# A 4096-point convolution beside a GELU layer: the second transform stage in 64 × 64 quarters of TensorE, the turn between the inverse stages as VectorE block transposes, by channel halves

## The chip, the core and the metric

One Trainium2 core runs one program. TensorE (PE; its weight loads are PEld), VectorE (DVE), ScalarE (ACT), GpSimd (POOL) and the DMA queues of SyncE (SP) and POOL run side by side and wait for each other through semaphores. The metric is the device time of the core in microseconds, median of the timed runs; the profile shows one execution, whose span is a little shorter than its time.

## The reference

Two branches on the same input `u` (2048 positions, 512 channels), mixed by a gate of each position:

```python
g = _sigmoid((x * gate_w).sum(-1, keepdims=True))
...
P = jnp.exp(logdA[:, :, None] * l[None, None, :])
K = jnp.einsum("dn,dnl,dn->dl", Cc, P, dB).real
...
Yf = Uf * Kf[None, :, :, :]
y = irfft2(Yf, (1, 2 * L))[..., :L].T + u * Dskip
...
h = _gelu(jnp.einsum("bsd,df->bsf", x, w1) + b1)
b = jnp.einsum("bsf,fd->bsd", h, w2) + b2
return g * a + (1 - g) * b
```

Branch `a` (its result is `y`) is a long convolution of every channel with 2048 taps `K`, which come from a state-space model with 128 states; it is done by transforms of length 4096. Branch `b` is a dense layer of width 1792 with GELU. Everything is float32. (The lines of `irfft2` and `_gelu` are shortened.)

## The kernel before

The program has two parts. `front` (lines 296 to 1023) holds three streams of work that a planner in Python lays out: `dense()` computes branch `b` in 16 blocks of 256 positions (two halves of the hidden width), `taps()` builds `K` in 16 chunks of 32 channels and takes each chunk through the first transform stage, and `signal()` does the same for `u` in 16 pieces. Each task has an engine, a cost and a due time (`vec`, `act`, `mm`, `move`, lines 303 to 318); `Plan.run` (line 216) turns them into one order for each engine by a list schedule, and the tasks are issued in that order. The constants at the top (`T_0`, `K_0`, `D_EV` and so on) are due times; `PS = (2, 3, 1, 2)` gives the PSUM banks of the accumulators `acc`, of the hidden block `ph`, of the tap chunk `pk` and of the first stage `pu`.

`first_stage` (line 369) splits its source into a high and a low part of reduced precision (`s1h` by ACT, `s1l` by DVE), and multiplies in two row halves of TensorE: six products of 512 columns (line 384) into two `pu` banks. For the signal ACT copies each bank to `st` and SP stores it to the DRAM buffer `t2_d`; for the taps ACT copies each to `sk` with a step (line 662), and after every fourth chunk eight DMAs store `sk` to `t2_d` in runs of 64 elements (line 677).

`conv` (line 1026) is issued in the order of the text, each engine in program order. It runs a loop over 32 frequencies `n`. One step:

- `fetch` (7 steps ahead): SP loads `t2` (512 KB, 128 partitions, taps and signal side by side), every fourth step the matrices `cc`.
- `forward` (2 ahead): two products with 128 × 128 weights and 512 columns, `p2k` for the taps, `p2u` for the signal.
- `factors` (1 ahead): ACT copies the real and the imaginary half of `p2k` into both halves of `kr` and `ki`, four copies of 64 × 512.
- `product`: DVE forms the complex product: two multiplications of 128 × 512, one difference and one sum of 64 × 512.
- `inverse`: one product of 128 × 128 and 512 columns into `pa`.
- `turn` and `settle` (1 behind): ACT copies `pa` to `sa`; SP stores it to the DRAM buffer `t4_d`; the partition of the next stage is another axis, so after a group of steps POOL collects the group from DRAM (or, for the last four steps, straight from `sa`) into the big tile `t3`, 32 rows of 512.

After the loop, `rest` multiplies what `front` left over of the dense branch (`late`), and 16 rounds of two products with `g1t` (128 × 64 weights, 512 columns, line 1137) turn `t3` into the output positions; DVE adds the gated result to the dense part `mo`, which was loaded from `out`, and SP stores it.

`front` uses the pools `kp` and `ps`; `conv` uses `fp` and `ps_f`, whose tiles take the same SBUF bytes and PSUM banks in the order of their first use, each tile waiting for the old tiles in its place. A tag with `bufs=n` has `n` places, and a new tile waits until all uses of the tile `n` before it are over.

Of the kernel before, what the change touches and what calls it, by code (L numbers as in the profile page):

```python
# [9 lines left out]
F32 = mybir.dt.float32  # L10
# [7 lines left out]
P = 128  # L18
# [29 lines left out]
PS = (2, 3, 1, 2)  # L48
# [21 lines left out]

GROUPS = ((0, 8, 0, 4), (8, 8, 1, 4), (16, 8, 2, 4), (24, 4, 3, 8), (28, 1, 7, 32), (29, 1, 15, 32), (30, 1, 23, 32), (31, 1, 31, 32))
# [9 lines left out]


def slot_q():
    return [32 + m if m < 32 else 63 - m for m in range(64)]


def k0_order():
    return [8 * (n % 4) + n // 4 for n in range(32)]
# [14 lines left out]
def constants():  # L103
# [6 lines left out]
    k0 = np.arange(32)  # L110
    p = np.arange(32)
    q = np.asarray(slot_q())
    k1 = np.arange(64)
    qn = np.arange(64)

    er, ei = om(4 * (64 * np.outer(p, k0) + 16 * p[:, None]))

    f1 = np.zeros((2, 32, 32, 2, 2))
    for i in range(2):
        f1[i, :, :, 0, i] = er  # L120
        f1[i, :, :, 1, i] = ei
    f1h, f1l = split12(np.concatenate([f1.reshape(64, P)] * 2, 0))


    g1 = np.zeros((2, 2, 32, 2, 32))
    for i in range(2):
        g1[i, 0, :, i] = er.T / L
        g1[i, 1, :, i] = ei.T / L
    g1 = g1.reshape(4, 32, 64)
    rows = np.zeros((P, 64))  # L130
    for first, count, at, step in GROUPS:
        for i in range(count):
            for j in range(4):
                rows[at + step * (4 * i + j)] = g1[j, k0_order()[first + i]]
    g1 = rows


    f2 = np.zeros((32, 2, 64, 2, 64))
    g2 = np.zeros((32, 2, 64, 64, 2))
    for k in range(32):  # L140
        er, ei = om(4 * (q[:, None] * k + 32 * np.outer(q, k1)) + q[:, None])
        f2[k, 0, :, 0], f2[k, 1, :, 0], f2[k, 0, :, 1], f2[k, 1, :, 1] = er, -ei, ei, er
        er, ei = om(4 * (qn[None] * k + 32 * np.outer(k1, qn)) + qn[None])
        g2[k, 0, :, :, 0], g2[k, 1, :, :, 0] = er, ei
        g2[k, 0, :, :, 1], g2[k, 1, :, :, 1] = -ei, er
    g2 = g2.reshape(32, P, 32, 2, 2).transpose(0, 1, 3, 4, 2)
    c2 = np.stack([f2.reshape(32, P, P), g2.reshape(32, P, P)], 1)
    c2 = c2[k0_order()].reshape(8, 4, 2, P, P).transpose(0, 3, 1, 2, 4)
    c1 = np.concatenate([f1h, f1l], 1)
    return (  # L150
# [1069 lines left out]
```

## Time and profile before

| | us |
|---|---|
| three timed runs: lowest, median, highest | 573.89, 574.33, 576.38 |
| the profiled execution | 573.42 |
| its span in the trace | 571.6 |
| PE busy | 538.8 (94%) |
| DVE busy | 476.7 (83%) |
| ACT busy | 415.8 (73%) |
| granted TensorE clock, mean | 0.976 |

Busy time is the union of the instructions of an engine; a float32 product of TensorE appears as two records. Rows of a group read: line, engine, operation, output and inputs, shape, count, then busy time, mean nanoseconds of one, and idle time before it with its releaser. Rows of the chain that ended last read: start, duration, engine, tile, line. Rows of a stretch read: the stretch, its length, busy time and count of each engine, granted clock, share of the DMA engines, GB/s.

### The profile page before, as it was taken

To read this page: it belongs to the slowest core of one execution; us is meant where nothing else is said; L and a number is where in the kernel's file an instruction comes from. 1 tells how busy PE (TensorE), PEld (TensorE's weight loads), DVE (VectorE), ACT (ScalarE), POOL (GpSimd) and SP (SyncE) were. 2 spreads that over 40 slices of the span, in tenths; PEclk is the share of its full clock that TensorE was granted. 3 is DMA by queue.
4 is the path that set the end of the run, shared out by engine and by line. 5 is a ranking of instruction groups with operands and counts; after the bars stand their busy time and mean duration, and the time that the engine had idled before them with its cause. 6 is when DMAs were issued, how large, how long until landed. Compare 5 with 4: busy or idle time off the path is not lost.

```text
span 571.6 us, 11723 instructions
## 1 busy us (share of the span) xinstructions
PE 538.8 (94%) x4554; PEld 407.9 (71%) x4554; DVE 476.7 (83%) x876; ACT 415.8 (73%) x702; POOL 32.2 (6%) x69
## 2 busy tenths in 40 slices
PE   7859999999999999999999999999998999999636
PEld 6728788888787888888888889898986333333412
DVE  5899998998889989898998898988613999999216
ACT  4998766799675799987678867376546999999100
POOL 2000000000000000000110111011100000000200
PEclk9959999999999999999999999999999999999959
DMA  8969644242774342558622339222259999999957
GB/s 254 309 202 325 215 139 160 101 130 84 233 233 143 117 131 93 159 183 216 172 76 38 94 92 187 74 39 76 38 126 338 368 311 406 452 349 349 280 123 285
DMA packets 77668, 110.01 MB, mean 192 GB/s; under 512 B 39030, under 2 KB 42234, under 8 KB 77500
## 3 DMA queue, kind: packets, MB, share of 16 engines
q1 hardware_dynamic: 71756, 88.41, 46.2%
q0 software_dynamic: 5856, 20.85, 14.8%
q8 instruction: 36, 0.59, 0.4%
q14 instruction: 20, 0.16, 0.1%
HBM read 63.62 MB, written 44.57 MB: 189 GB/s over the span
## 4 chain that ended last, share of the span: by engine, by line
PE 82%; DMA 7%; ACT 5%; DVE 3%; issue 2%; SPq 0%; POOL 0%; POOLq 0%; DVEq 0%
PE pk L643 11%; PE acc L901 9%; PE ph L853 9%; PE ph L855 8%; PE ph L854 8%; PE acc L903 8%; PE acc L902 8%; PE pa L1076 6%; PE pu L384 4%; PE p2k L1049 4%; PE p2u L1050 4%; DMA t<-sa 3%; PE pb L1137 3%; DMA t_d<-sa 1%; DMA y<-in_w_dram 1%
## 5 line engine op out<-in xcount | busy, mean ns | idle before, releaser
L853 PE MATMUL ph<-xh,wh 128*128 128x256 f32 x448 | 128.0, 286 | 1.9 <-DVE wh L732 1.1
L855 PE MATMUL ph<-xh,wl 128*128 128x256 f32 x448 | 127.1, 284 | 0.6 <-DVE wl L736 0.5
L854 PE MATMUL ph<-xlo,wh 128*128 128x256 f32 x448 | 126.6, 283 | 0.0
L853 PEld LDWEIGHTS ph<-xh,wh 128*128 128x128 f32 x448 | 85.1, 190 | 8.0 <-issue 4.1
L901 PE MATMUL acc<-wh,hh 128*128 128x512 f32 x210 | 87.8, 418 | 0.6 <-ACT hh L873 0.6
L854 PEld LDWEIGHTS ph<-xlo,wh 128*128 128x128 f32 x448 | 85.1, 190 | 1.7
L855 PEld LDWEIGHTS ph<-xh,wl 128*128 128x128 f32 x448 | 85.1, 190 | 1.5 <-DVE wl L736 1.5
L902 PE MATMUL acc<-wl,hh 128*128 128x512 f32 x210 | 83.1, 396 | 0.0
L903 PE MATMUL acc<-wh,hl 128*128 128x512 f32 x210 | 83.1, 396 | 0.0
L870 ACT ACTIVATE ph<-ph,b1t 128x256 f32<-128x256 f32 x112 | 50.6, 452 | 28.3 <-PE ph L855 26.5
L643 PE MATMUL pk<-y,xc 128*32 128x64 f32 x2048 | 61.5, 290 | 0.0
L643 PEld LDWEIGHTS pk<-y,xc 128*32 128x32 f32 x2048 | 57.2, 136 | 4.0 <-issue 2.5
L901 PEld LDWEIGHTS acc<-wh,hh 128*128 128x128 f32 x210 | 39.8, 190 | 19.9 <-issue 11.9
L883 DVE TENSOR_TENSOR hl<-ph,hh 128x512 fp32r<-128x512 f32 (+1 forms) x62 | 38.2, 618 | 14.1 <-ACT hh L873 13.8
L903 PEld LDWEIGHTS acc<-wh,hl 128*128 128x128 f32 x210 | 39.8, 190 | 10.0 <-DVE hl L883 1.1
L607 DVE TENSOR_TENSOR y<-y,ea 128x64 f32<-128x64 f32 (+4 forms) x80 | 45.3, 566 | 0.4
L662 ACT COPY sk<-pu 128x512 f32<-128x512 f32 x32 | 33.9, 1130 | 15.4 <-PE pu L384 15.3
L902 PEld LDWEIGHTS acc<-wl,hh 128*128 128x128 f32 x210 | 39.9, 190 | 5.8
L873 ACT CAST hh<-ph 128x512 fp32r<-128x512 f32 (+1 forms) x62 | 33.0, 532 | 10.9 <-PE acc L902 9.1
L452 DVE TENSOR_TENSOR xt<-xc,zz 128x256 f32<-128x256 f32 (+2 forms) x48 | 37.2, 775 | 1.9 <-ACT xc L578 1.6
L1058 ACT COPY kr<-p2k 64x512 f32<-64x512 f32 x64 | 37.0, 578 | 2.1 <-PE p2k L1049 1.7
L1059 ACT COPY ki<-p2k 64x512 f32<-64x512 f32 x64 | 37.2, 581 | 1.2
(137 smaller groups left out, 952.9 us busy)
## 6 DMA issues: line engine op xcount, KB each, us to landing
t<-t_d SPq DMA_DIRECT2D x32, 512.0 KB, 7.6
t_d<-st SPq DMA_DIRECT2D x32, 256.0 KB, 3.2
t_d<-sk SPq DMA_DIRECT2D x32, 256.0 KB, 4.3
t_d<-sa SPq DMA_DIRECT2D x28, 256.0 KB, 5.5
mo<-out_dram SPq DMA_DIRECT2D x9, 512.0 KB, 9.0
ld<-in_xt_dram SPq DMA_DIRECT2D x16, 256.0 KB, 4.2
xh_d<-xh SPq DMA_DIRECT2D x8, 512.0 KB, 4.3
xl_d<-xlo SPq DMA_DIRECT2D x8, 512.0 KB, 6.2
```

What stands on the lines that cost most here:

```text
L452: vec(2 * m, lambda: vv.tensor_mul(t, a, br), due, [ka, *kb], [kt])
L607: nc.vector.tensor_mul(both(n, 64 - 3 * n, n), both(0, 64 - n, n), an)
L643: nc.tensor.matmul(pks[q][32 * j : 32 * j + 32, gg], x[:, r, :, ch], y[:, r, :, ch], start=(r == 0), stop=(r == 1), skip_group_check=True,)
L853: nc.tensor.matmul(p, h, xh[xk][:, d], start=(d == 0), stop=False)
L854: nc.tensor.matmul(p, h, xlo[xk][:, d], start=False, stop=False)
L855: nc.tensor.matmul(p, lo, xh[xk][:, d], start=False, stop=(d == 3))
L870: nc.scalar.activation(phs[q][:, n], phs[q][:, n], AF.Gelu_apprx_tanh, bias=b1t[:, f : f + 1])
L883: nc.vector.tensor_sub(lo, phs[q][:, 0:nf], hi.bitcast(F32))
L901: nc.tensor.matmul(a, h, wh[1][w], start=start, stop=False)
L902: nc.tensor.matmul(a, h, wl[1][w], start=False, stop=False)
L903: nc.tensor.matmul(a, l, wh[1][w], start=False, stop=(j == 3))
L1059: nc.scalar.copy(ki[h : h + 64], pk[64:128])
```

## The change

The second transform stage, the product, the inverse and the last stage are rearranged.

- The 4096-point transform is split the other way round: the first stage now has 64 frequencies, the second 32 points, so that real and imaginary parts of 32 points are 64 rows. All 64 × 64 products of `conv` use one of four quarters of TensorE: two row halves, two column halves.
- `conv` runs 16 steps: two channel halves `f` of 256 channels, eight groups `m` of four frequency pairs. A step loads 1 MB of `t2` with four DMAs of 32 partitions each, and in the first eight steps 0.46 MB of the matrices `ca`, which now stay.
- `taps` (8 products of 256 columns) and `signal` (two times 8: the second time with weights moved by 32 columns, which gives real and imaginary part exchanged) go into whole banks; `factors` is two copies, `product` two multiplications each time. The sums of the complex product are made by `inverse`, which adds up two products in PSUM: 16 products.
- `collect` copies the result into `ta[f]`; there is no store to DRAM and no collecting. `turn` is a block transpose on DVE, 64 channels at once (2048 elements per partition): for the first half four of them lie in the loop, behind steps 7, 8, 11, 12; for the second half four stand after the loop.
- The last stage of the first half is done in the loop (`mix_first`, two behind each of the steps 9, 10, 13, 14): ACT scales by the gate, POOL adds to `out` in DRAM. The second half is done at the end, with DVE and `mo` as before, but with 256 columns.
- `rest` stands between the loop and the last four turns.
- In `front`, the first stage of the taps becomes `first_stage_taps`: 24 products of 256 columns in four row tiles into three `pu` banks and the `pk` bank itself, four strided copies of 256 elements; `PS` is `(2, 2, 1, 3)`. The stores to `t2_d` have runs of 256 (signal) and 128 (taps) elements. The due times are unchanged.

The diff, cut to its core:

```diff
-PS = (2, 3, 1, 2)
+PS = (2, 2, 1, 3)
...
+        def first_stage_taps(src, key, due, evac):
+            hi, lo, reads = split1(src, key, due)
+            banks = [(pus[q], ("pu", q)) for q in (take("pu", N_PU) for _ in range(3))]
+            banks.append((src, key))
...
+                todo = [(b, w, x) for b in range(2) for w, x in ((0, hi), (0, lo), (1, hi))]
+                for i, (b, w, x) in enumerate(todo):
+                    for j, (z, _) in enumerate(banks):
+                        r = slice(32 * j, 32 * j + 32)
+                        nc.tensor.matmul(
+                            z[:, 0:HD], c1t[r, 2 + 2 * b + w], half(x, r, b), start=(i == 0), stop=(i == 5)
+                        )
...
+        ca = pool.tile([P, 32, 224], F32, name="ca", bufs=1)
+        ta = [pool.tile([P, 32, HD], F32, name=f"ta{f}", bufs=1) for f in range(2)]
+        tb = pool.tile([P, 32, P], F32, name="tb", bufs=1)
...
+        def fetch(s):
+            f, m = divmod(s, 8)
+            if f == 0:
+                nc.sync.dma_start(ca[:, 4 * m : 4 * m + 4], c2[m])
+            t2s[s] = pool.tile([P, 4, 2, HD], F32, tag="t2", name=f"t2{s}", bufs=3)
+            for i in range(4):
+                nc.sync.dma_start(
+                    t2s[s][32 * i : 32 * i + 32], t2_d[f, m, i].rearrange("n q w d -> q n w d")
+                )
...
+        quarters = [(n, h, h, h ^ n) for n in range(2) for h in range(2)]
+        def forward(s, w, at, zs):
+            for p in range(2):
+                cs = slice(HD * p, HD * p + HD)
+                for n, h, r, c in quarters:
+                    j = 2 * p + n
+                    nc.tensor.matmul(
+                        zs[h][part(c), cs], ca[part(r), 4 * (s % 8) + j, at : at + 64],
+                        t2s[s][part(r), j, w], start=True, stop=True,
+                    )
...
+        def product(s, i):
+            for h, z in enumerate(pus.pop((s, i))):
+                w = pool.tile([P, D], F32, tag=f"w{i}{h}", name=f"w{s}{i}{h}", bufs=2 - i)
+                nc.vector.tensor_mul(w, z, fac[s][h])
...
+        def inverse(s):
+            pas[s] = [bank("pa", f"pa{s}{r}", 2) for r in range(2)]
+            for p in range(2):
...
+                            nc.tensor.matmul(
+                                pas[s][r][part(h), cs],
+                                ca[part(r), 4 * (s % 8) + 2 * p + n, 96 + 64 * i : 160 + 64 * i],
+                                prod[s, i][h][part(r), cs], start=(i == 0), stop=(i == 1),
+                            )
...
+        def turn(dst, d, src, e, n):
+            nc.vector.transpose(
+                dst[:, :, d : d + n].rearrange("p q d -> p d q"),
+                src[:, :, e : e + n].rearrange("p n d -> p d n"),
+            )
...
+        def mix_first(d, t):
+            z = bank("pb", f"pb{d}{t}", 1)
+            last(z, tb, 2 * t, 4, P)
+            ob = pool.tile([P, 4, P], F32, tag="ob", name=f"ob{d}{t}", bufs=2)
+            for i in range(4):
+                nc.scalar.mul(ob[:, i], z[:, P * i : P * i + P], gate[:, 0, t + i : t + i + 1])
...
+        for s in range(-1, 16):
+            if s < 15:
+                if s + 1 == 0:
+                    taps(1)
+                    factors(1)
+                signal(s + 1, 0)
+                product(s + 1, 0)
+                if 0 <= s and s + 2 < 16:
+                    taps(s + 2)
+                    factors(s + 2)
+                signal(s + 1, 1)
+                product(s + 1, 1)
+                if s >= 0 and s + 3 < 16:
+                    fetch(s + 3)
...
+            if s >= 0:
+                inverse(s)
+                collect(s)
+            if s in (7, 8, 11, 12):
+                i = (s + 1) % 2
+                turn(tb, 64 * i, ta[0], 64 * (i + 2 * (s // 10)), 64)
+            if s in (9, 10, 13, 14):
+                d = P * (s // 12)
+                for t in (0, 4) if s in (9, 13) else (8, 12):
+                    mix_first(d, t)
+        rest()
+        for d in range(0, HD, 64):
+            turn(ta[0], d, ta[1], d, 64)
+        for t in range(0, 16, 2):
+            z = bank(("pa", "pu")[t // 2 % 2], f"pz{t}", 2 + t // 2 % 2)
+            last(z, ta[0], 2 * t, 2, HD)
...
+                nc.vector.scalar_tensor_tensor(
+                    mo[:, i % 8], z[:, HD * (i - t) : HD * (i - t) + HD], gate[:, 0, i : i + 1], mo[:, i % 8],
+                    ALU.mult, ALU.add,
+                )
```

The tile `pk` has two banks, `pu` three (two taken by each `signal`), `pa` two, `pb` one. `w0` has two buffers per half, `w1` one.

More of the change, by code (lines that the diff above doesn't have):

```diff
@@ L129, in constants @@
[L129 to L145, printed above, removed]
@@ L150, in constants @@
+    c2 = c2.reshape(8, 4, P, 224).transpose(0, 2, 1, 3)
     return (
@@ L1092, in turn @@
[L1092 to L1108 removed]
+        t2s, pks, pus, fac, prod, pas = {}, {}, {}, {}, {}, {}
@@ L1109, in rest @@
                 first = s not in accs
-                last = not any(e[0] == s for e in late)
                 if first:
-                    accs[s] = ps.tile([P, D], F32, tag="pk", name=f"acc{s}", bufs=2)
+                    accs[s] = bank("pk", f"acc{s}", 2)
                 ss = slice(s * P, (s + 1) * P)
```

258 lines of the change are left out of this document (120 added, 138 removed).

## The prediction

> **What bounds the kernel now.** I read the page's head first, then the busy time by stretch of the span, then the chain that ended last.
>
> ```profile
> span 571.6 us, 11723 instructions
> core 0: us, PE busy (x) PEld busy (x) DVE busy (x) ACT busy (x) POOL busy (x), PEclk, DMA share, GB/s
> 0.00:436.30 436.30, 423.10 (x4256) 361.13 (x4256) 377.20 (x729) 325.88 (x542) 27.42 (x61) 0.98 0.52 150
> 436.30:523.10 86.80, 85.51 (x183) 32.28 (x184) 79.04 (x119) 82.96 (x148) 1.59 (x3) 1.00 1.00 379
> 523.10:551.60 28.50, 14.69 (x52) 9.19 (x51) 8.49 (x13) 6.92 (x13) 3.24 (x5) 0.82 0.91 241
> 551.60:571.60 20.00, 15.48 (x64) 5.29 (x64) 12.01 (x16) 0.00 (x0) 0.00 (x0) 0.92 0.64 236
> ```
>
> Four stages. The planned front (436 us) is TensorE's: 423 busy. In the loop over 32 frequencies (86.8 us, 2.7 each) PE, ACT and DVE are all over 90% busy. Then 28.5 us in which the turned tile is collected, and 20 us of last stage and stores. The chain says the same:
>
> ```profile
> 436.86 1.11 PE p2k L1049 x2
> 437.99 0.58 ACT kr L1058
> ...
> 441.82 0.69 DVE v L1071
> 442.56 1.13 PE pa L1076 x2
> ...
> 453.65 1.03 PE pa L1076 x2
> 454.69 0.86 PE p2k L1049 x2
> ...
> 523.58 7.91 DMA t_d<-sa
> ...
> 533.99 17.05 DMA t<-sa
> ...
> 551.67 15.50 PE pb L1137 x64
> ...
> 567.19 0.75 DVE mo L1139
> ```
>
> A float32 product of 512 columns is two records, 0.86 us. A wait from PE to ACT costs about 0.2 (the product at 436.86 streams until 437.8, the copy starts at 437.99), one from DVE to PE 0.05 (442.51 to 442.56). From the last inverse (523.1) to the end are 48.5 us, 25 of them DMA. That is what the change can win; the loop is the other half of its account.
>
> **The change part by part: the front.** Where the operands of a product cover part of the array, these rows count:
>
> ```profile
> 305.05 3.84 PE L643 MATMUL pk<-y,xc 128*32 128x64 f32 x128
> 415.90 0.90 PE pu L384 x6
> 551.60:554.90 3.30, 3.23 (x8) 1.12 (x10) 0.52 0.47 151
> ```
>
> L384 alternates two row halves: six products of 512 columns in 0.90. The tap first stage becomes 24 products of 256 columns over four row tiles: the same 0.9 if four run together, 0.7 more if two (times 16: 0 to +11 us). I take 0, as L384's two halves do run together: one product of 512 columns alone takes 0.23 (rows in the tail's part), six 1.4. ACT gets four strided copies of 256 for two of 512, about 0.3 us more per chunk, 5 in all, hidden in ACT's idle 110 us of this stage. The tap stores move the same bytes in runs twice as long; the last ones lie beside the last dense products, and uncovered would cost one landing, some 5 us. Two `ph` banks instead of three:
>
> ```profile
> L870 ACT ACTIVATE ph<-ph,b1t 128x256 f32<-128x256 f32 x112 | 50.6, 452 | 28.3 <-PE ph L855 26.5
> L873 ACT CAST hh<-ph 128x512 fp32r<-128x512 f32 (+1 forms) x62 | 33.0, 532 | 10.9 <-PE acc L902 9.1
> L883 DVE TENSOR_TENSOR hl<-ph,hh 128x512 fp32r<-128x512 f32 (+1 forms) x62 | 38.2, 618 | 14.1 <-ACT hh L873 13.8
> ```
>
> A bank is drained in 2 × 0.45 + 0.53 + 0.62 = 2.1 us; the block of the next bank gives 24 products, 2.9 us, and the plan has other products to put in. Nothing to +6 us (sixty-four blocks, a tenth of a microsecond each), and the third `pu` bank works the other way; I take +1: the front ends at 437.
>
> **Start of the loop.** In the new pool `ca`, `ta`, `tb` fill the first 108 KB, so the second and third `t2` buffer lie where `xh1`, `xlo1` and `wh0` lay: their loads wait for the last hidden product, where eight were loaded ahead.
>
> ```profile
> 435.09 0.28 PE L855 MATMUL ph<-xh,wl 128*128 128x256 f32 x1
> 431.43 2.22 SPq L1039 DMA_DIRECT2D t<-t_d  x4
> ```
>
> A first load took 431.43 to 436.86, 5.4 us. So `taps(1)` starts at 435.4 + 5.4 + 1 = 441.8, not at 437; PE stands about 4 us with `signal(0)` queued behind. Then, by the prices worked out next: taps to 442.7, signal to 443.6, its product to 444.5, second signal to 445.4, and 0.9 until a bank is free: the first full step starts at 446.
>
> **One step of sixteen** is 8 + 16 + 16 products of 64 × 64 and 256 columns. One is 0.43 alone. Two column halves run together at full rate (L1137: 32 products of 512 columns in 15.5 us, the first four in 3.3 at a clock of 0.52, so 28 in 12.2, 0.436 each where one alone takes 0.86), two row halves as well (L384); four column strips finish 64 products in 3.84 us where 64 × 0.107 would be 6.8. I take four together: 0.44 per four, bounds 0.43 (exact) and 0.86 (two). So signal 0.88, taps 0.88, signal 0.88, inverse 1.75: PE 4.4 per step. The rest by
>
> ```profile
> L1068 DVE TENSOR_TENSOR w<-p2u,kr 128x512 f32<-128x512 f32 x32 | 22.1, 692 | 6.7 <-ACT kr L1058 3.1
> L1094 ACT COPY sa<-pa 128x512 f32<-128x512 f32 x32 | 18.7, 585 | 3.0 <-PE pa L1076 1.5 <-DMA t_d<-sa 0.7
> ```
>
> DVE 4 × 0.69 = 2.8 and ACT 4 × 0.585 = 2.3 per step: two steps of old work, 5.5 and 5.9, are halved. But the step is a ring. Second signal: starts when the first product has freed its bank, 0.88 + 0.2 + 0.69 + 0.05 = 1.82; inverse ends 1.82 + 0.88 + 1.75 = 4.45. `w1` has one buffer, which the inverse still reads when the next second product is due: that product starts 0.2 after the inverse, frees a `pu` bank 0.69 + 0.05 later, and only then may PE begin the next signal: +0.94. The step is **5.39 us**. Fifteen: 446 + 4.45 + 14 × 5.39 = 526 for the end of `inverse(14)` without the extras.
>
> Loads: 1.05 MB a step and 0.46 MB of `ca` in the first eight; at the loop's 379 GB/s 4.0 us, hidden under 5.39.
>
> **The turns.** No row shows a block transpose. One moves 2048 elements per partition, with steps of 512 to 1024 bytes on both sides.
>
> ```profile
> L505 DVE TENSOR_SCALAR xv<-xt 128x896 f32<-128x896 f32 x4 | 2.5, 623 | 0.7 <-ACT xt L493 0.7
> L620 DVE TENSOR_TENSOR y<-y,tt 128x2048 f32<-128x2048 f32 x16 | 36.6, 2286 | 0.0
> L406 ACT COPY st<-pu 128x512 f32<-128x512 f32 x32 | 17.3, 589 | 8.6 <-PE pu L384 8.4 <-DMA t_d<-st 0.3
> L662 ACT COPY sk<-pu 128x512 f32<-128x512 f32 x32 | 33.9, 1130 | 15.4 <-PE pu L384 15.3
> ```
>
> Lowest: L505's pace, 1.4. Contiguous: 2.3. L662 writes with a 256-byte step and takes 1.92 times L406: 2.29 × 1.92 = 4.4; reading and writing one after the other 8.8. I take **4.4**, since the step is what L662 has in common with it.
>
> Four turns are in the loop. Each starts behind the last product of its step (1.57 after the inverse), and the next step's first product is queued behind it: second signal at 1.57 + 4.4 + 0.69 + 0.05 = 6.7 after the inverse instead of 0.94 + 1.82 = 2.76. +3.95 each, 15.8.
>
> **Last stage, first half.** In steps 9, 10, 13, 14 two `mix_first` stand behind the inverse on PE. One is 8 products of 128 columns in two column halves, 0.85. The single `pb` bank makes the second wait for ACT: collect (1.4 after the inverse), then four scalings.
>
> ```profile
> L922 ACT ACTIVATE io<-acc,gate 128x512 f32<-128x512 f32 x30 | 20.5, 691 | 17.0 <-PE acc L903 16.3 <-DVE gate L796 0.7
> ```
>
> L870's 256 elements in 0.452 and L922's 512 in 0.691 give 0.93 ns an element: 0.33 at 128, four 1.3. So the second block runs from 2.75 to 3.6. The next signal was due at 0.94: +2.66, three times 8.0; step 14's stands before `inverse(15)`, 3.6 + 1.75. End of the last inverse: 526 + 15.8 + 8.0 + 5.35 = 555.1 (before 523.1).
>
> **The tail.** What goes is 28.5 us of bounce. What is late next is DVE: `rest()` puts 42 products on PE,
>
> ```profile
> 303.57 0.40 PE L901 MATMUL acc<-wh,hh 128*128 128x512 f32 x1
> ...
> 304.74 0.39 PE L903 MATMUL acc<-wh,hl 128*128 128x512 f32 x1
> ```
>
> (six starts, 0.23 apart: 9.8 us), its two DVE sums stand in front of the four turns: 10.5. Turns 4 × 4.4 = 17.6. PE, idle meanwhile, restarts at half clock as at 551.6 (8 records in 3.3 us, clock 0.52). Last stage: 32 products of 256 columns, 3.4 cold plus 24 × 0.214 = 8.5; DVE
>
> ```profile
> L1139 DVE SCALAR_TENSOR_TENSOR mo<-pb,gate,mo 128x512 f32<-128x512 f32 x16 | 12.0, 750 | 16.5 <-DMA mo<-out_dram 14.8 <-PE pb L1137 0.3
> ```
>
> at 256 elements 0.48 (L1068 and L620 differ by 1.04 ns an element), 16 of them, the later ones back to back: 10.4 in all. Stores and end 3.7 (567.9 to 571.6). Tail 0.2 + 10.5 + 17.6 + 10.4 + 3.7 = 42.4 against 48.5.
>
> **Sum.** 555.1 + 42.4 = 597.5; the profiled execution took 1.8 us more than its span (573.4, which is 0.9 under the median of 574.3): **599 us**, 26 more. The ledger: front and start +10, loop +22, tail -6.
>
> **Rivals.** (1) The turns run at the contiguous pace, 2.3: 8.4 less in the loop and 8.4 in the tail: **582**. For it: L620 streams 2048 elements at that pace; against it: L662. The Trainium skill, "Vector Engine (DVE) Microarchitecture Reference", § 3.8, says that a block transpose sustains one element per cycle per lane; that is this rival, and no run here shows a transpose. (2) The `t2` loads, now four of 32 partitions each, are slow and set the step.
>
> ```profile
> t<-t_d SPq DMA_DIRECT2D x32, 512.0 KB, 7.6
> t<-t_d POOLq DMA_DIRECT2D x4, 10.2
> ```
>
> The POOL row's groups are 32 partitions, 2.1 MB: 206 GB/s. So 5.1 a step, 6.2 with `ca`: start +2.5, five steps of +0.8: **606**. Against it: that row shares the DMA engines with the loop's other transfers. The Trainium skill, "SBUF — State Buffer", § Door 1, measured 189 GB/s into partitions 0 to 31 and 328 into all at 1 MiB; by it a step's load is an estimate of 5.5 us and the time about 609. (3) The other side: PE stays the loop's bound, because the ring's wait for `w1`, the turns and the `pb` wait hide under its 4.4 us: from 446, 15 × 4.38 + 6.8 + 1.75 = 74.3 to the last inverse, 520; **565**. It decides once 28 of those 35 us are hidden. For it: DVE and ACT are each under two thirds busy; against: one buffer of `w1`, one bank of `pb`. (4) The quarters do not run four together: two at a time add 4.3 to each step, less what the turns then hide: about **657**.
>
> **How the numbers follow.** Forecast 0.47, (1) 0.16, (2) 0.17, (3) 0.12, (4) 0.08. Range: (4) and half of (3) left out; the top takes in 11 us of tap products and 6 of the `ph` bank on the forecast: 566 to 622. The forecast alone: 588 to 612. Under 571.5 (0.5%, what a measurement can tell): most of (3) and a quick front, 0.13; within: between (3) and (1), 0.08; slower 0.79.
>
> **What would show it.** Product records of the quarters in clusters of four starts, 0.22 apart; gaps of about a microsecond on PE before each first signal, released by DVE; turns of 4.4; POOL out of the chain, DVE's turns in it; the front's end within 3 us of 436. Wrong if a turn is near 2, if PE shows no gap at `w1`, or if loads release the taps.

## The result and the profile after

The changed kernel takes 627.88 us (median of 4 runs, 627.22 to 630.08) where the kernel before takes 575.08 beside it: a ratio of 1.0924, with a 95% interval of 1.0885 to 1.0963. It is 53 us slower, where the forecast of 599 was some 25 above the kernel before, and the time lies 6 us above the top of the range.

The span of the profiled execution is 625.5 us. Its stretches, cut at its own borders: the end of the hidden products, the inverse of the last step without a turn, the last inverse. They answer to the four stretches of before, with the same columns.

```profile
0.00:451.40 451.40, 430.67 (x4548) 369.67 (x4548) 379.51 (x728) 328.79 (x573) 27.39 (x61) 0.98 0.49 147
451.40:514.90 63.50, 45.26 (x707) 28.58 (x706) 23.03 (x37) 19.17 (x37) 0.00 (x0) 0.95 0.97 214
514.90:585.60 70.70, 49.08 (x703) 31.10 (x703) 35.20 (x34) 23.99 (x60) 9.30 (x8) 0.90 0.64 126
585.60:625.50 39.90, 18.16 (x106) 13.28 (x106) 24.00 (x22) 2.02 (x4) 2.60 (x3) 0.79 0.33 71
```

The front is 15 us longer, and TensorE stands in it for 20.7 us where it stood 13.2. In the loop, where three engines were over 90% busy, none is over 72% now. The first half of the loop has the DMA engines busy all the time at 214 GB/s; the loop before moved 379 at the same share. The second half waits for something else, since the share falls to 0.64. Only the tail is shorter, 40 us for 48.5.

A stretch of the front in which the changed kernel stands, and the same stretch of the kernel before:

```profile
200.00:240.00 40.00, 36.35 (x410) 29.86 (x413) 33.58 (x64) 31.97 (x59) 1.20 (x3) 0.91 0.28 88
```

```profile
200.00:240.00 40.00, 40.00 (x446) 33.93 (x446) 36.95 (x67) 38.84 (x68) 2.39 (x6) 1.00 0.37 112
```

It stands 3.7 us of these 40, and the granted clock falls to 0.91: slow products behind a pause count as busy. That is a part of why the front's busy time is 7.6 us up too.

The groups that carry the change, from the groups of the changed kernel, and behind them the same two dense groups of the kernel before:

```profile
L864 PE MATMUL ph<-xh,wh 128*128 128x256 f32 x448 | 130.6, 292 | 7.6 <-DVE hl L894 5.0 <-ACT wh L745 1.4 <-DVE wh L743 1.1
L912 PE MATMUL acc<-wh,hh 128*128 128x512 f32 x210 | 88.0, 419 | 4.4 <-ACT hh L884 4.3
L1099 DVE TENSOR_TENSOR w<-pu,k 128x512 f32<-128x512 f32 x64 | 41.2, 688 | 71.7 <-PE pa L1111 47.0 <-PE pu L1073 24.7
L1073 PE MATMUL pk<-t,ca 64*64 64x256 f32 x256 | 24.8, 397 | 11.3 <-DMA t<-t_d 11.3
L1124 DVE STREAM_TRANSPOSE tb<-ta 128x2048 f32<-128x2048 f32 x4 | 16.8, 4195 | 0.0
L1124 DVE STREAM_TRANSPOSE ta<-ta 128x2048 f32<-128x2048 f32 x4 | 16.2, 4152 | 0.0
```

```profile
L853 PE MATMUL ph<-xh,wh 128*128 128x256 f32 x448 | 128.0, 286 | 1.9 <-DVE wh L732 1.1 <-ACT wh L734 0.8
L901 PE MATMUL acc<-wh,hh 128*128 128x512 f32 x210 | 87.8, 418 | 0.6 <-ACT hh L873 0.6
```

Read the idle column. The hidden products (L864) wait for `hl`, whose reading frees the `ph` bank, and the output products (L912) for `hh`; before, these two groups stood 1.9 and 0.6 us, and for weights in the first. `product` (L1099) waits 47 us for the inverse: the single `w1`. The taps' products (L1073 `pk`) wait 11.3 us for loads. A turn takes 4.2 us.

The steps of the loop can be read from ScalarE's copies `ta<-pa` (`collect`), one row of two copies for each inverse and 0.15 us behind its end. In the timeline of ScalarE:

```profile
469.54 1.07 ACT L1120 COPY ta<-pa 128x512 f32<-128x512 f32 x2 [1.51 <-PE pa L1111]
...
503.84 1.07 ACT L1120 COPY ta<-pa 128x512 f32<-128x512 f32 x2 [1.52 <-PE pa L1111]
...
509.39 1.07 ACT L1120 COPY ta<-pa 128x512 f32<-128x512 f32 x2 [1.73 <-PE pa L1111]
...
514.93 1.07 ACT L1120 COPY ta<-pa 128x512 f32<-128x512 f32 x2 [1.73 <-PE pa L1111]
```

The inverse of step 0 ends 18 us behind the front; five steps take 34.3 us together, 6.86 each; steps 6 and 7 take 5.55 and 5.54. So the account, with the forecast's own terms:

| | forecast | measured | more |
|---|---|---|---|
| end of the front | 437 | 451.4 | 14.4 |
| from there to the end of inverse 0 | 13.5 | 18.0 | 4.5 |
| steps 1 to 5 | 27.0 | 34.3 | 7.3 |
| steps 6 and 7 | 10.8 | 11.1 | 0.3 |
| steps 8 to 15 (turns, last stage) | 66.9 | 70.7 | 3.8 |
| tail | 42.4 | 39.9 | -2.5 |

Together 28 us above the 597.5 of the forecast: 625.5.

Where the loop loses is seen in the timeline of TensorE (start, duration, line, count, and in brackets the idle time and its releaser):

```profile
451.37 1.09 PE L1073 MATMUL pk<-t,ca 64*64 64x256 f32 x16
455.86 1.08 PE L1073 MATMUL pk<-t,ca 64*64 64x256 f32 x2 [3.39 <-DMA t<-t_d]
458.25 1.55 PE L1073 MATMUL pk<-t,ca 64*64 64x256 f32 x11 [1.31 <-DMA t<-t_d]
...
470.19 0.87 PE L1073 MATMUL pu<-t,ca 64*64 64x256 f32 x11 [0.78 <-DVE w L1099]
...
472.68 0.87 PE L1073 MATMUL pk<-t,ca 64*64 64x256 f32 x11 [1.40 <-DMA t<-t_d]
...
512.75 1.88 PE L1111 MATMUL pa<-w,ca 64*64 64x256 f32 x28
...
520.89 1.55 PE L1073 MATMUL pu<-t,ca 64*64 64x256 f32 x11 [3.30 <-DVE w L1099]
...
522.25 3.61 PE L1111 MATMUL pa<-w,ca 64*64 64x256 f32 x28
```

The stretch of that last inverse, with the granted clock as the third number from the end:

```profile
522.25:525.86 3.61, 3.61 (x40) 1.96 (x32) 0.00 (x0) 0.00 (x0) 0.00 (x0) 0.50 0.57 129
```

`taps(1)` waits twice for its load (451.4 to 458.3). Each first signal (470.19) stands 0.8 us for the product behind the inverse, and each `taps` of the first half 1.0 to 1.4 more for its load (472.68). Behind the first turn the second signal stands 3.3 us, and then the products themselves are slow: the same 28 records of an inverse take 3.61 us where they took 1.88, at a granted clock of 0.50. The step behind the third turn (8.87 us) has the same pause and no slow products; the other three take 10.4 to 11.4.

### The profile page after: what moved, and what is told of

It is laid out like the page before. It is cut to its first block, busy times and chain, and to the rows that moved or that the text cites. A ratio compares the mean times of both kernels' runs of the same rounds, so it can differ in the third digit from the quotient of the medians.

```text
span 625.5 us, 14613 instructions
## 1 busy us (share of the span) xinstructions
PE 543.2 (87%) x6058; PEld 442.6 (71%) x6058; DVE 461.7 (74%) x820; ACT 374.0 (60%) x673; POOL 39.3 (6%) x71
## 5 line engine op out<-in xcount | busy, mean ns | idle before, releaser
L864 PE MATMUL ph<-xh,wh 128*128 128x256 f32 x448 | 130.6, 292 | 7.6 <-DVE hl L894 5.0
L864 PEld LDWEIGHTS ph<-xh,wh 128*128 128x128 f32 x448 | 86.2, 192 | 15.6 <-DVE hl L894 5.9
L1099 DVE TENSOR_TENSOR w<-pu,k 128x512 f32<-128x512 f32 x64 | 41.2, 688 | 71.7 <-PE pa L1111 47.0
L912 PE MATMUL acc<-wh,hh 128*128 128x512 f32 x210 | 88.0, 419 | 4.4 <-ACT hh L884 4.3
L1073 PE MATMUL pu<-t,ca 64*64 64x256 f32 x512 | 52.1, 410 | 23.5 <-DVE w L1099 23.5
L912 PEld LDWEIGHTS acc<-wh,hh 128*128 128x128 f32 x210 | 40.3, 192 | 20.1 <-issue 6.8
L1073 PEld LDWEIGHTS pu<-t,ca 64*64 64x64 f32 x512 | 26.1, 141 | 39.7 <-DVE w L1099 33.8
L1120 ACT COPY ta<-pa 128x512 f32<-128x512 f32 x32 | 17.2, 589 | 46.2 <-PE pa L1111 46.2
L1111 PE MATMUL pa<-w,ca 64*64 64x256 f32 x512 | 41.1, 413 | 0.0
```

What stands on the lines that cost most here:

```text
L864: nc.tensor.matmul(p, h, xh[xk][:, d], start=(d == 0), stop=False)
L912: nc.tensor.matmul(a, h, wh[1][w], start=start, stop=False)
L1073: nc.tensor.matmul(zs[h][part(c), cs], ca[part(r), 4 * (s % 8) + j, at : at + 64], t2s[s][part(r), j, w], start=True, stop=True,)
L1099: nc.vector.tensor_mul(w, z, fac[s][h])
L1111: nc.tensor.matmul(pas[s][r][part(h), cs], ca[part(r), 4 * (s % 8) + 2 * p + n, 96 + 64 * i : 160 + 64 * i], prod[s, i][h][part(r), cs], s ...
```

## The experiments

My theory after this look: four causes that hardly touch each other. The front lies in an order that was laid out for three hidden banks; the loads are slow because of their form (rival 2 of the forecast), and late at the start because of their place; the ring through `w1` costs about a microsecond a step; a turn costs more than its 4.2 us because TensorE's clock falls behind it. The rivals stand with each run. All times are medians beside runs of the kernel before on the same chip, ratios with their 95% interval.

### The front: the banks alone

```diff
 (the kernel before)
-PS = (2, 3, 1, 2)
+PS = (2, 2, 1, 3)
```

> The kernel before with the changed kernel's PSUM banks, PS = (2, 2, 1, 3), and nothing else: its loop, its tail and its first stage of the taps are the old ones. If the front's 16 us (last hidden product at 451.4 in place of 435.4) come from the bank that the hidden block gave up, under due times that were not changed, this kernel's last hidden product ends at 448 to 455 as well and the time is 588 to 595. If they come from the new first stage of the taps (its products, its four copies, the tap bank that it holds), the front ends within 3 us of 435 and the time is 574 to 577.

593.1 us, ratio 1.0326 (1.0215 to 1.0437). In this kernel's view of the tile `ph` (count, shortest, median and longest duration, first and last start), the last hidden product:

```profile
L855 PE MATMUL ph<-xh,wl x448: 274/283/415, 7.6 to 454.3; 128*128 128x256 f32 x150
```

The same row of the changed kernel:

```profile
L866 PE MATMUL ph<-xh,wl x448: 274/283/416, 8.0 to 451.2; 128*128 128x256 f32 x150
```

The last start is 454.3, where it is 451.2 in the changed kernel and 435.1 before. So the new first stage of the taps isn't needed to explain the loss; the banks alone cost more than the whole front lost.

The second half of the question is which bank: the hidden one that went or the first-stage one that came.

```diff
 (the kernel before)
-PS = (2, 3, 1, 2)
+PS = (2, 2, 1, 2)
```

> The kernel before with PS = (2, 2, 1, 2): one hidden bank less, and the third first-stage bank that the run before also gave is not there. If the missing hidden bank alone shifts the order, the front ends at 446 to 455 and the time is 585 to 593. If it was the third first-stage bank, which lets those products be put ahead of hidden ones, the front ends within 4 us of 435: 574 to 579.

585.96 us, ratio 1.0176 (1.0136 to 1.0216). The same row of this kernel's view of `ph`:

```profile
L855 PE MATMUL ph<-xh,wl x448: 274/283/416, 7.6 to 446.4; 128*128 128x256 f32 x150
```

The missing hidden bank makes 11.3 us of it, the additional first-stage bank another 7.9: with the old due times even a bank more does harm. That is the sign of an order, not of a resource, and the traces show the other order. When the last chunk of tap products starts, TensorE has started 416 of the 448 products of the row `ph<-xh,wh` in the kernel before, 392 in this kernel and 396 in the changed one: the hidden products have fallen behind the others.

### The front: other due times

```diff
 (the changed kernel)
-T_0 = 23.08
-T_MLP = 408.54
+T_0 = 22.23
+T_MLP = 399.98
...
-T_KG = 374.6
+T_KG = 391.83
...
-D_EV = -45.11
-D_H = -39.23
+D_EV = -56.93
+D_H = -62.48
...
```

> The changed kernel with other due times of the front alone (T_0, T_MLP, K_0, T_KG, U_0, the D_ constants and the three warps); its banks PS = (2, 2, 1, 3), its first stage of the taps and everything in conv stay. If the front's 16 us lie in an order that was laid out for three hidden banks, and not in the bank or the new first stage themselves, the last hidden product ends at 435 to 441 in place of 451.4 and the time is 612 to 618. If two hidden banks cannot feed TensorE in any order, the front still ends after 446 and the time is above 621.

630.5 us, ratio 1.0953 (1.0919 to 1.0988): half right. The front did come down, with the same banks and the same first stage, as the view of `ph` has it:

```profile
L866 PE MATMUL ph<-xh,wl x448: 274/283/415, 7.9 to 439.7; 128*128 128x256 f32 x150
```

That is 11.5 us earlier than in the changed kernel, and 428 of the 448 products of `ph<-xh,wh` stand ahead of the last tap chunk. But the gain was lost at once: the time is above the 612 to 618 that I expected. The first load of the loop needs the last tap store in DRAM. In the timelines of this kernel's SP queue and of TensorE:

```profile
433.29 6.04 SPq L689 DMA_DIRECT2D t_d<-sk  x8
```

```profile
451.96 1.08 PE L1073 MATMUL pk<-t,ca 64*64 64x256 f32 x2 [11.98 <-DMA t<-t_d]
```

The eight stores are issued from 433.3, 6.3 us later than in the changed kernel (427.0); from the first of them to the first product of the loop 18.7 us pass, and TensorE stands for 12. My due times had been chosen for the end of the products alone. A front ends when its last result can be loaded, and that is a second end to watch. The groups say what the missing bank still costs in this order: the hidden products still wait 5.8 us for `hl` in this kernel, while the wait of L912 for `hh` is gone (4.4 to 0.0).

### The loads: form and place

```diff
 (the changed kernel)
-        rows = t2_d.rearrange("f m i n q w d -> (m i n) q w f d")
+        rows = t2_d.rearrange("f m n i q w d -> (m n i) q w f d")
...
-            for i in range(4):
-                nc.sync.dma_start(
-                    t2s[s][32 * i : 32 * i + 32], t2_d[f, m, i].rearrange("n q w d -> q n w d")
-                )
+            nc.sync.dma_start(t2s[s], t2_d[f, m].rearrange("n i q w d -> (i q) n w d"))
```

(and the columns of the first stage's matrix in the same new order)

> The changed kernel with one t2 load of 128 partitions and 1 MB a step in place of four of 32 partitions and 256 KB; the bytes and the length of a run (2 KB) stay. If the 32-partition form is what makes the first steps wait (rival 2), inverse to inverse falls from 6.5 to 7.1 us in steps 1 to 5 to the 5.55 of steps 6 and 7, 6.6 us in all, and the start gives back 2 to 4: 616 to 620. If it is the bytes (1.05 MB of t2 and 0.46 MB of ca a step) or the moment at which a load is issued, the steps stay at 6.5 or more and the time at 625 to 629.

619.14 us, ratio 1.0779 (1.067 to 1.0889). The copies `ta<-pa` of this kernel:

```profile
468.85 1.07 ACT L1117 COPY ta<-pa 128x512 f32<-128x512 f32 x2 [1.51 <-PE pa L1108]
...
474.35 1.07 ACT L1117 COPY ta<-pa 128x512 f32<-128x512 f32 x2 [1.73 <-PE pa L1108]
...
496.53 1.07 ACT L1117 COPY ta<-pa 128x512 f32<-128x512 f32 x2 [1.73 <-PE pa L1108]
```

Every step takes 5.5 now, from the first on; the start gave back only 1.6 us, less than the 2 to 4 that I had thought. The stretch from 465 to 500, in this kernel and in the changed one:

```profile
465.00:500.00 35.00, 30.32 (x516) 18.14 (x512) 16.75 (x26) 13.62 (x26) 0.00 (x0) 1.00 0.76 262
```

```profile
465.00:500.00 35.00, 24.62 (x416) 16.33 (x408) 14.02 (x23) 10.74 (x20) 0.00 (x0) 1.00 1.05 224
```

The same bytes in the same runs of 2 KB: over 128 partitions the DMA engines move 262 GB/s and are busy 0.76 of the time, since they now wait for the loop; in pieces of 32 partitions they are full at 224. This edit changes two things, the partitions of one load and its size. The start of the changed kernel tells them apart: there the dense weights come in loads of 256 KB with runs of 2 KB too, but over 128 partitions each, among a few other loads.

```profile
3.00:9.00 6.00, 4.30 (x29) 3.91 (x28) 4.24 (x14) 3.67 (x8) 0.29 (x2) 1.00 1.03 349
```

The engines are full there as well, at 349 GB/s. So it is the 32 partitions and not the 256 KB, and rival 2's mechanism is shown. By the Trainium skill, "SBUF — State Buffer", § Door 1, partitions 0 to 31 reach half of the memory's DMA ports, and neighbours that differ by 32 reach the same ones; the full share at 224 GB/s here, beside 349 and the 379 of the loop before, agrees with it. Its 189 GB/s is for one transfer alone; this mixture with `ca` (128 partitions) came to 224.

The other half is where the buffers lie.

```diff
 (the changed kernel)
+        t2s = {
+            s: pool.tile([P, 4, 2, HD], F32, tag="t2", name=f"t2{s}", bufs=3) for s in range(3)
+        }
         ca = pool.tile([P, 32, 224], F32, name="ca", bufs=1)
...
```

> The changed kernel with the three t2 buffers placed first in the new pool, ahead of ca, ta and tb, so that they no longer lie where the hidden block's inputs lay; the amount and the form of the loads stay. If the start waits for that place, the loads of steps 1 and 2 are issued at about 440 in place of 451, taps(1) follows the last hidden product at once, and the first inverse ends 9 to 11 us after the front in place of 17.8; the loads are then ahead by two steps and part of the 6.6 us of steps 1 to 5 goes too: 612 to 620. If the start is set by the rate of the loads, the first inverse stays 14 us or more behind the front and the time is above 622.

621.4 us, ratio 1.0819 (1.0719 to 1.0919). In its timeline of TensorE the loop's first products:

```profile
451.78 1.09 PE L1077 MATMUL pk<-t,ca 64*64 64x256 f32 x16
453.56 1.36 PE L1077 MATMUL pk<-t,ca 64*64 64x256 f32 x13 [0.69 <-ACT k L1096]
```

`taps(1)` waits for no load; inverse 0 ends 11.6 us behind the front, 6.3 less. The place theory holds for the start, and the place is worth more there than the form (1.6 us). My hope for the steps behind it failed: they stay at 6.6 to 7.2, and the time is just above the 612 to 620 that I expected. Being ahead at the start does not help where the rate is short in every step.

### The ring through w1

```diff
 (the changed kernel)
-w = pool.tile([P, D], F32, tag=f"w{i}{h}", name=f"w{s}{i}{h}", bufs=2 - i)
+w = pool.tile([P, D], F32, tag=f"w{i}{h}", name=f"w{s}{i}{h}", bufs=2)
```

> The changed kernel with two buffers of w1 in place of one, so that the second product of a step no longer waits for the inverse before it. If that ring sets the steps that no load and no turn holds, inverse to inverse falls there from 5.55 to 4.5, by 1.05 in some eight to nine steps, and nothing in steps 1 to 5: 617 to 621. If the ring closes elsewhere (the three pu banks, the copy of the taps), the steps stay within 0.3 of 5.55 and the time at 624 to 629.

616.62 us, ratio 1.0736 (1.0639 to 1.0832). Its copies `ta<-pa`, in the timeline of ScalarE:

```profile
469.30 1.07 ACT L1120 COPY ta<-pa 128x512 f32<-128x512 f32 x2 [1.48 <-PE pa L1111]
...
504.23 1.07 ACT L1120 COPY ta<-pa 128x512 f32<-128x512 f32 x2 [2.84 <-PE pa L1111]
...
508.76 1.07 ACT L1120 COPY ta<-pa 128x512 f32<-128x512 f32 x2 [1.71 <-PE pa L1111]
```

Where no load holds a step, it takes 4.53, the 4.4 of TensorE's own work. The five steps under the loads take 34.9 us, as before (34.3): a shorter ring only makes DMA the one that is waited for. The runs with the 128-partition loads and with two `w1` buffers together show that steps 1 to 5 were bound by loads and steps 6 and 7 by the ring. The wait of `product` for the inverse, 47.0 us in the changed kernel, is gone in this one. The time is where I expected it, but partly for another reason: I had counted 1.05 us in eight or nine steps. Steps 6 and 7 give that; 9.1 of the gain lie in the steps behind the second and the fourth turn (5.8 and 5.9 us for 10.4 each), since the second product no longer waits for the inverse and the second turn of a pair follows it at once.

### The pauses behind the turns

```diff
 (the changed kernel)
+                if s in (8, 12):
+                    rest((s - 8) // 4)
                 signal(s + 1, 1)
...
-        rest()
         for d in range(0, HD, 64):
```

(`rest(k)` now does one block of 128 positions, 21 products into the `pb` bank; ACT scales it, POOL adds it to `out`)

> The changed kernel with the rest of the dense branch moved from behind the loop into two of the four pauses that the turns make on TensorE: 21 products each (4.9 us) into the pb bank between taps and the second signal of the steps with the turns 1 and 3, scaled by ACT and added to out by POOL; DVE's two sums in front of the last turns go. Both theories: the tail falls from 40 to 29.5 to 30.5. If the slow product records behind the turns (inverse 3.6 us in place of 1.9) are a clock that falls because TensorE stood still, then behind the two filled pauses signal and inverse run at 0.88 and 1.9, and behind the two left empty they stay slow; the steps with filler cost at most 1 us more than before for the 4.9 us of products, and the time is 614 to 618. If the slow records have another cause (DVE's transposes taking the banks or the memory), they stay slow behind the filled pauses too, the products come on top, and the time is 618 to 622.

619.13 us, ratio 1.0752 (1.0709 to 1.0795). In its timeline of TensorE, behind the first, filled pause and behind the second, empty one:

```profile
524.40 1.91 PE L1111 MATMUL pa<-w,ca 64*64 64x256 f32 x32
...
532.33 1.55 PE L1073 MATMUL pu<-t,ca 64*64 64x256 f32 x11 [3.27 <-DVE w L1099]
...
533.68 4.04 PE L1111 MATMUL pa<-w,ca 64*64 64x256 f32 x31
```

The slow records need a TensorE that stood: with products in the pause the inverse takes 1.91 behind a turn of the same length, without them 4.04. The fourth pause, empty too, was not followed by slow products (2.10 for the same 31 records), which neither theory had. Over the runs the picture holds: of eighteen empty pauses of 3.3 us (this kernel, the changed one, and the runs with other loads, other place and other due times) fifteen are followed by slow products, and of six filled ones (here and in the next two runs) none. So the transposes are not the cause. The Trainium skill, "TensorE: Matmul & The Clock Gate", § Part 1, has the clock fall to half after an idle window of about 3.4 us that runs freely. The traces differ from that a little: the pauses here are 3.3 us, and pauses of 2.3 us in the next two runs are followed by slow products too, in three of four cases. So TensorE need not stand for the whole window. Whether slow products follow may hang on where the window lies against the pause; no run tests that. The 42 products came cheap: the two filled steps take 0.7 us more together (10.5 each, for 11.4 and 8.9), while the tail falls by 8.2 us (10 were expected). The second filled step took 1.6 us more than before, which is above the 1 us that I had allowed. The time, 619.1, lies in the range that I had given to the other theory; what speaks against that theory is the product records, not the time.

### All repairs, and the start once more

The next run is the changed kernel with the edits of five runs together: other due times, one load a step, `t2` first, two buffers of `w1`, the rest in the pauses.

> All repairs so far in one: one t2 load of 128 partitions a step, t2 first in the pool, two buffers of w1, the rest in the pauses, and the other due times. If they are independent, front 435 to 441, start 10 to 12, steps without turn or last stage 4.5, the loop's other half as in the run with two w1 buffers (about 60), tail 30: 566 to 577, about the time of the kernel before or a little under. If TensorE itself or the memory takes the place of the waits, steps stay at 5 us or more, and the time is 580 to 595.

596.89 us, ratio 1.0352 (1.0306 to 1.0398). That is above both ranges that I had given. The steps came out (4.5 to 5.0 from the first on), and so, nearly, did the tail, 31.7. Two parts did not. The start has the fault of the run with other due times: 25.4 us from the front to inverse 0 (440.60 to 451.30 TensorE stands). And steps 8 to 15 take 66.1 us where about 60 were expected. The run with two `w1` buffers alone has 60.5 there: with the rest in the first pause of a pair, the steps behind the second turns take 8.9 and 8.7 us again, where they had come down to 5.8 and 5.9. So the causes do touch each other: beside that run the tail is 9.1 us shorter, and steps 8 to 15 are 5.6 longer. The due times were chosen once more, with the last tap store as a second end:

```diff
 (all repairs)
-K_0 = 26.08
+K_0 = 35.89
...
-D_KP = -88.12
+D_KP = -98.84
...
-D_EV = -56.93
-D_H = -62.48
+D_EV = -35.94
+D_H = -18.19
...
-                    256,
+                    660,
                     lambda: nc.scalar.copy(
                         sk[:, :, c, j].rearrange("p s g -> p g s"),
```

> The run with all repairs once more, with a third set of due times, chosen so that the last chunk of the taps is stored earlier (the set before ended TensorE's front at 440.6, but its last tap store went out at 439.3 in place of 432.2, and the loop stood 10.7 us for its loads), and with the taps' four copies entered in the plan at what they take, 0.65 us. If the front's time is a matter of order alone, products and last store can both be early: last hidden product at 438 to 444, the first inverse 10 to 13 us behind it in place of 25.4, everything after as in that run (113.7 to the last inverse, tail 31.7): 578 to 590. If products and stores can only be traded against each other, front end and start together stay at 463 to 466 and the time at 592 to 597.

584.22 us, ratio 1.0192 (1.0156 to 1.0228). The last stores leave from 421.6; the last hidden product starts at 442.0, and the copies give inverse 0 at 11.6 us behind the front. Its stretches, cut as above:

```profile
0.00:442.30 442.30, 425.88 (x4548) 367.13 (x4552) 378.03 (x728) 327.17 (x572) 27.45 (x61) 0.99 0.51 153
442.30:485.70 43.40, 40.08 (x690) 28.52 (x694) 23.59 (x37) 19.10 (x37) 0.00 (x0) 1.00 0.84 284
485.70:551.20 65.50, 55.44 (x768) 38.18 (x760) 35.40 (x34) 25.43 (x62) 10.99 (x10) 0.97 0.64 147
551.20:582.90 31.70, 9.81 (x68) 6.25 (x64) 23.15 (x20) 1.07 (x2) 0.94 (x1) 0.65 0.32 79
```

Against the changed kernel: 9 us less in the front, 20 in the loop's first half, 5 in its second, 8 in the tail. The second half now stands out: its eight steps, with turns and last stage, take 65.5 us where eight of 4.53 would take 36.

### The turns in pieces

```diff
 (the run before)
-            if s in (7, 8, 11, 12):
-                i = (s + 1) % 2
-                turn(tb, 64 * i, ta[0], 64 * (i + 2 * (s // 10)), 64)
-            if s in (9, 10, 13, 14):
-                d = P * (s // 12)
-                for t in (0, 4) if s in (9, 13) else (8, 12):
-                    mix_first(d, t)
+            if 11 <= s < 15:
+                mix(0, 0, 4 * (s - 11))
+            if 7 <= s < 15:
+                turn(0, 32 * (s - 7), 32)
```

(`turn` works in place; `rest`, the other four blocks of the first half and the second half, in two parts of 128 channels, follow the loop)

> The same front and loads, and the turns taken apart: in place (ta itself, no tb) and in eight pieces of 32 channels, one behind the second product of each of the steps 7 to 14, a last-stage block of 128 channels behind each of the inverses 11 to 14, everything else of the first half's last stage and the rest of the dense branch behind the loop beside the last four turns, the last 256 channels in two halves. If a turn costs only because four of them stand in one lump of 4.2 us in front of a product, and the second block of a pair only because it waits for the one pb bank, the loop's 16 steps take 4.5 to 5.7 each, 76 to 82 from the first inverse to the last in place of 113.7, tail 28 to 33: 545 to 558, faster than the kernel before. If DVE's pieces (2.1 us beside 2.7 of products) or TensorE's clock set the steps, they take 6 or more each in the second half, and the time is 560 to 575.

570.33 us, ratio 0.9952 (0.9924 to 0.998): a little faster than the kernel before, by a margin that hardly matters. In the timeline of VectorE a turn of 32 channels between the products of two steps:

```profile
491.24 1.29 DVE L1099 TENSOR_TENSOR w<-pu,k 128x512 f32<-128x512 f32 x2 [0.59 <-PE pu L1073]
492.45 2.27 DVE L1125 STREAM_TRANSPOSE ta<-ta 128x1024 f32<-128x1024 f32 x1
494.60 1.26 DVE L1099 TENSOR_TENSOR w<-pu,k 128x512 f32<-128x512 f32 x2
```

Much of it fits into the time in which VectorE waits anyway: a step with such a piece takes 5.2 us where one without takes 4.53 (the first, whose turn waits for the copy into `ta`, takes 6.8). From inverse 0 to inverse 15 the loop takes 75.3 us (453.6 to 528.9), a little under the 76 to 82 expected; but part of the last stage and the rest now stand behind it. The tail took 39.7 where 28 to 33 were expected, so that the time is not in the range of 545 to 558. The end of the chain that ended last:

```profile
549.90 6.50 POOL out_dram L1144 x5
556.40 1.29 POOLq L1284
```

All arithmetic is done at 555.0 and the last addition to `out` is issued by 557.7; the span ends at 568.6. The additions, each 256 KB in runs of 512 bytes, are the likely cause. The last run puts less on that queue:

```diff
 (the run before)
+        for k, t in enumerate((0, 4, 8, 12)):
+            mix(0, P, t, *(("pa", 2), ("pu", 3))[k % 2])
         rest(0)
         rest(1)
...
+        mix(1, P, 12)
+        for k, t in enumerate((0, 4, 8)):
...
```

> The run with the turns in pieces once more, with another order behind the loop: the four blocks of the first half's second 128 channels come before the rest of the dense branch and take turns in the pa and pu banks, and of the last 128 channels only one block of four positions is still added to out by POOL, the other three by DVE into mo with SP storing. In the run before, the last inverse stood at 528.9, the last scaling at 555.0, and the end at 568.6: the additions to out by POOL landed last, six of them issued behind 549.9. If it is these that make the end late, it comes 6 to 10 us earlier, at 558 to 563, and the time is 560 to 565. If the stores of SP or the amount of bytes hold the end as long, it stays within 3 us: 567 to 572.

566.82 us, ratio 0.9854 (0.9833 to 0.9876): the fastest of all, 1.5% under the kernel before, though 2 us above what I expected. The tail fell to 35 us, 4.6 less where 6 to 10 were expected; arithmetic ends at 554.2, and 11 us still pass until the span's end. The time lies just under the 567 to 572 of the other theory, so that the additions set the end alone is not shown.

## Why the prediction was wrong

**The front** is the step that failed: "Nothing to +6 us (sixty-four blocks, a tenth of a microsecond each), and the third `pu` bank works the other way; I take +1". The front ended 14.4 us later than that. I priced a bank by how long it takes to drain and how much other work there is to put in between. What I left out is that the order is a list laid out from due times, and the same due times with other banks give another list: 396 products of `ph<-xh,wh` ahead of the last tap chunk where there were 416. "The plan has other products to put in" is true only if the due times put them there. With the same banks and other due times the front ends at 440.0 or 442.3, 4.6 or 6.9 us above before, so that 9 to 11 of the 16 us were the list's. Whether the bound of 6 for the bank itself was fair stays open. The third `pu` bank worked against the kernel, not for it (454.3 against 446.4). For the tap first stage I took no cost, and no run shows one: the banks alone give the whole loss.

**The loads** "hidden under 5.39" were the second error, and rival 2 was right in mechanism and low in price: I gave it 2.5 us at the start and five steps of 0.8. The five steps took 1.5 more each, and the other form of the load takes all of that away. The start was 4.5 late, but the form gives back only 1.6 of it. There the place of the buffers weighs more: I had the wait for the last hidden product, but not that the products behind it run slow (the 11 records of `taps` at 458.25 take 1.55 us, those at 472.68 0.87), and I reckoned it from a front that ends at 435.4 though the same sum had 437. I had worked it out for 6.2 us a step, from a row at 206 GB/s for `t2` and 379 for `ca`; the mixture took 6.86. The evidence against it, that the POOL row shared its DMA engines with other loads, was a reason to doubt the row's size, not its sign.

**The ring** was right: 5.55 for the 5.39 of the forecast, with the wait behind the inverse seen at 0.78 for the 0.94 of the sum; its undoing gives 4.53, against the 4.4 that I had for TensorE alone. Four quarters do run together (an inverse of 16 products 1.9, forecast 1.75), so rival 4 falls.

**The turns** at 4.2 (forecast 4.4) were right, and rival 1 falls with them. The reason that I gave, the step of the access, wasn't tested: no run has a turn without a step, so the nearness of the number may be luck. What the turns do to the loop was 3.7 us too small over the four: I had the second signal late by the turn, and forgot that TensorE mostly comes back from such a pause at half its clock, although the same sum uses this for the tail. Where it didn't, the step took 8.87 us, under the 9.34 of the sum. **The last stage**'s waits (2.66 each) were right within 0.2: the three steps with them take 24.3 us, forecast 24.2.

**The tail** was 2.5 us shorter than forecast, in the same order of events.

**Rival 3**, that TensorE hides all of it, is what the repaired loop comes near to: 4.53 a step, once the ring, the loads and the lumps of VectorE are gone. It wasn't to be had from the change alone. The range was too narrow because the front's upper bound left out the order. Its top doesn't follow from its terms either: 11 and 6 on the forecast of 599 give 616, not 622.

What stays open: the best front found here ends at 440.0 to 442.4 and not at 435.4. Whether better due times would close that with two hidden banks, or whether it is the price of the bank, wasn't tried; nor were the new due times with the old three banks.

## What to carry to other kernels

Where a planner lays out an order, a changed count of buffers is a changed order: look first at whether its constants were chosen for the old count, and watch every result that the next stage loads, not only the busiest engine. Price a load by the partitions that one transfer covers, and a lump on an off-path engine by what is queued behind it: a turn of 4.2 us made its step 3.3 to 5.9 us longer, a piece of half the size 0.7 (the first 2.3). A pause on TensorE can cost twice, once as a pause and once as half clock behind it, so work from the tail that fits there is cheap as long as the pause is there; here another repair had shortened the second pause of each pair, and the two gains did not add up.

## What the hardware showed that I had not expected

Additions into DRAM by POOL's queue seem slow to drain; no run has them alone. In the run with the turns in pieces six of 256 KB were issued from 549.9, and 13.6 us passed between the end of all arithmetic and that of the span; its tail had the DMA engines busy at 0.81 for 100 GB/s:

```profile
528.90:568.60 39.70, 21.05 (x234) 18.12 (x234) 19.30 (x12) 13.24 (x44) 15.24 (x13) 0.87 0.81 100
```

A block transpose with steps of 512 to 1024 bytes costs about 2 ns an element in each partition: 4.15 us for 2048 from one tile to another, 2.27 for 1024 in place. And a copy of ScalarE that writes with a step of 512 bytes is slower than one of twice the size that writes long runs (589 ns for 512 in the row of L406 that the forecast shows); the groups of the changed kernel:

```profile
L674 ACT COPY sk<-pu 128x256 f32<-128x256 f32 x48 | 27.5, 658 | 11.2 <-PE pu L398 8.0 <-PE pk L398 3.2
```
